# A convolution and a routed FFN on one core: weights ahead of the first rows, small scale operations on GpSimd, routing of the first chunks sooner

## The chip, the core and the metric

The kernel runs on one core of one Trainium2 chip. The core has TensorE (PE, matrix products), VectorE (DVE), ScalarE (ACT) and GpSimd (POOL), each with a queue that it works off in order, and SyncE (SP), which issues most DMA transfers. PSUM is where TensorE leaves its products, SBUF the memory that all engines work in. The metric is the device time of one execution in microseconds (us); less is better.

## The reference

A softmax over 7 weights per head forms a causal convolution of x; its output goes through a layer of 8 experts of which each row uses one.

```python
# attention-like convolution: B, S, D = 8, 3584, 192; 8 heads; K = 7
w = np.exp(weight_gen - weight_gen.max(-1, keepdims=True)); w /= w.sum(-1, keepdims=True) + 1e-9
out = np.einsum('bshk,bskhg->bshg', w, x_unf)      # 7 shifted rows of x per row
x = out.reshape(28672, 192)
# experts: w1 (8, 192, 1024), w2 (8, 1024, 192)
logits = x @ w_gate
expert_idx = np.argmax(logits, axis=1)
gate_w = softmax(logits)[row, expert_idx]
for e in range(8):
    h = np.maximum(x[expert_idx == e] @ w1[e], 0)
    out[expert_idx == e] = gate_w * (h @ w2[e])
```

## The kernel before

**Chunks.** The rows are taken in 16 chunks of up to 14 tiles of 128 rows. conv(c) forms a chunk on VectorE by multiplications (L358) and additions (L363) of two SBUF operands; soft_a and soft_b (L302 to L341) do its softmax, size_a (L312, ScalarE) and size_b (L322, GpSimd) find a power of two by which the chunk is scaled. The rows are then split into two fp16 halves: the upper by ScalarE (tops, L372), the lower by VectorE (halves, L384). TensorE transposes them (turn, L398; ScalarE copies them out, L399) and multiplies them by the router's weights (products, L407).

**Routing.** route1(s) (VectorE, L419 to L437) picks each row's expert and leaves counts per expert in cnt; its first operation, fac (L419), is the factor that undoes the scaling. counts(s) issues ScalarE's Exp (L445) and TensorE's two sums of counts (L446, L447). route2(s) (VectorE, L468 to L482) computes pos, the place of each row in a list sorted by expert, and its 14 scatters (L457, GpSimd, DMA_INDIRECT scr<-rows,pos) write the rows to a buffer in DRAM. VectorE then builds small tables of blocks (L494 to L534).

**Preparation of the experts' weights.** Each expert's weights are scaled by powers of two from their size and split into fp16 parts: sq (L184, ScalarE, squares), total (L232, TensorE, sums over partitions), scales (L234: scale_of, L171 to L180, four small operations on VectorE: eb, ei, ws, wi), high (L244 si, L246 wt, ScalarE), low (TensorE L256, L257, ScalarE L258) and store (SyncE, L266 to L273, to wsc in DRAM). prep_units() lists these units in order, and prepare(t, ta) issues those that are due by time t.

**FFN.** The sorted rows are worked through in blocks of 256 rows, 7 blocks per stage; stage s can begin when the scatters of some chunk have landed. load() has SyncE issue the first weights (L563, L564), the transposed rows x (L571, which waits for the stage's scatters), mt (L579) and the second weights (L590). Per block TensorE does the first products (L611 to L615), ScalarE takes hh (L618), VectorE the remainder hl (L628; in early stages ScalarE, L626), TensorE the second products (L644), ScalarE scales them to y (L651), and GpSimd writes y to the output by two indirect DMAs (L652, DMA_INDIRECT out_dram<-y,mt).

**Order.** VectorE, ScalarE, TensorE and SyncE work in the order in which two coroutines issue instructions: produce() (chunks, routing, preparation) and consume() (FFN). Each holds an estimated time; t and ta are those of VectorE and ScalarE, avail[s] is the time from which a stage's blocks may be issued, and whichever coroutine is behind goes next. The tables FIRST, SECOND, THIRD, EARLY and STEADY say behind which of a chunk's 13 convolution operations (-1 to 13) each part of the work on the chunk before is issued; SECOND holds for the work on chunk 1, THIRD for chunk 2. GpSimd's order is made by the scheduler from what was issued, with priorities. In load(), the first block of all took x ahead of its first weights, the others behind them.

Of the kernel before, what the change touches and what calls it, by code (L numbers as in the profile page):

```python
# [7 lines left out]
F32 = mybir.dt.float32  # L8
# [4 lines left out]
ALU = mybir.AluOpType  # L13
AX = mybir.AxisListType

P = 128
# [23 lines left out]
THIRD = dict(tops=-1, halves=0, turn=1, per=2, products=3, route1=5, counts=6, route2=7, soft_a=8, soft_b=10, size=11)  # L40
SECOND = dict(tops=-1, halves=-1, turn=-1, per=6, products=-1, route1=-1, counts=-1, route2=0, soft_a=6, soft_b=10, size=8)
# [38 lines left out]
def conv_moe_kernel(ctx: ExitStack, tc: tile.TileContext, x, wgen, wg_in, w1, w2, out):  # L80
# [90 lines left out]
    def scale_of(ss, s_out, i_out, by=GP):  # L171


        n = ss.shape[1]
        eb = small.tile([P, 4], F32, name="eb", bufs=4)
        ei = small.tile([P, 4], I32, name="ei", bufs=4)
        by.tensor_scalar(out=eb[:, 0:n], in0=ss.bitcast(I32), scalar1=11.0 * 2 ** 23, scalar2=-(2.0 ** -24), op0=ALU.max, op1=ALU.mult)
        by.tensor_scalar(out=ei[:, 0:n], in0=eb[:, 0:n], scalar1=190 - 2.0 ** -8, scalar2=None, op0=ALU.add)
        by.tensor_scalar(out=s_out.bitcast(I32), in0=ei[:, 0:n], scalar1=2.0 ** 23, scalar2=None, op0=ALU.mult)
        by.tensor_scalar(out=i_out.bitcast(I32), in0=s_out.bitcast(I32), scalar1=-1.0, scalar2=254.0 * 2 ** 23, op0=ALU.mult, op1=ALU.add)  # L180
# [39 lines left out]
    def prep_units():  # L220
# [13 lines left out]
        def scales(e):  # L234
            with tc.high_priority(offset=PRIO3):
                scale_of(sqs.pop(e)[0][:, 0:2], ws[:, 2 * e:2 * e + 2], wi[:, 2 * e:2 * e + 2], V)
# [85 lines left out]
    def size_b(c):  # L322
        ll = tin[c]["ll"]
        sx = small.tile([P, 4], F32, name="sx", bufs=4)
        tin[c]["new"] = ll[:, 0:1]
        if WID[c] > 7:
            GP.tensor_tensor(out=ll[:, 3:4], in0=ll[:, 0:1], in1=ll[:, 1:2], op=ALU.add)
            tin[c]["new"] = ll[:, 3:4]
        GP.tensor_tensor(out=sx[:, 0:1], in0=tin[c]["new"], in1=tin[c - 1]["new"] if c else ll[:, 2:3], op=ALU.add)
        scale_of(sx[:, 0:1], sx[:, 1:2], sx[:, 2:3])  # L330
        tin[c]["sx"] = sx
# [81 lines left out]
    def route1(s):  # L413
# [3 lines left out]
        with tc.high_priority(offset=PRIO2):  # L417
            fac = small.tile([P, 1], F32, name="fac")
            V.tensor_scalar(out=fac, in0=d["sx"][:, 2:3], scalar1=wi[:, 2 * E:2 * E + 1], scalar2=None, op0=ALU.mult)  # L419
# [21 lines left out]
    def counts(s):  # L441
        d = seg[s]
        d["pc"] = pc = d["pl"][:, 496:512]
        with tc.high_priority(offset=PRIO2):
            A.activation(out=d["lg"], in_=d["lg"], func=AF.Exp, scale=d["fac"])  # L445
            PE.matmul(pc[:, 0:E], lhsT=tri, rhs=d["cnt"], start=True, stop=True)  # L446
            PE.matmul(pc[:, E:16], lhsT=ones, rhs=d["cnt"], start=True, stop=True)  # L447

# [103 lines left out]
    def load(s, tb, g, bs):  # L552
# [8 lines left out]

        def firsts():
            SP.dma_start(out=wt[:, F:4 * F], in_=wsc[bass.ds(ev, 1), :, F:4 * F].rearrange("o p c -> p (o c)"))  # L563
            SP.dma_start(out=wt[0:64, 0:F], in_=wsc[bass.ds(ev, 1), 0:64, 0:F].rearrange("o p c -> p (o c)"))  # L564

        ahead_of_rows = bool(loaded)
        if ahead_of_rows:
            firsts()
# [7 lines left out]
        if not ahead_of_rows:  # L576
            firsts()
# [117 lines left out]
    def produce():  # L695
# [23 lines left out]
        for c in range(nchunk + 1):  # L719
# [4 lines left out]
            for o in range(-1, OPS + 1):  # L724
# [63 lines left out]
                if o == -1 and c == 2:  # L788
                    ta = prepare(ta + 1.0, ta)
# [4 lines left out]
                if o == at_o["counts"] and c:  # L794
                    counts(c - 1)
# [7 lines left out]
                ta = prepare(t - 2.5 if c == 1 and o > 10 else t, ta)  # L803
# [110 lines left out]
```

## Time and profile before

| | |
|---|---|
| time, median of 3 runs | 1248.54 us (1246.06 to 1250.6) |
| the profiled execution | 1246.52 us, of which the span 1244.7 us |
| PE busy | 1124.1 us, 90% of the span |
| DVE busy | 1061.7 us, 85% |
| POOL busy | 809.0 us, 65% |
| ACT busy | 705.7 us, 57% |
| DMA | 323.03 MB, 260 GB/s on average |

The busy shares are means over very different stretches: preparation and the first chunks up to about 158 us, then convolution and FFN side by side, and from about 967 us on mostly FFN. Starts are counted from the beginning of the span. A row of a timeline gives start, duration, engine, line of the kernel, operation, what it writes and reads, and in brackets how long the engine was idle ahead of it and whose work ended that.

### The profile page before, as it was taken

The page shows a single profiled execution, that of the slowest core. Times are in us where ns is not written, and L with a number is a line of the kernel's source. Part 1 is how long each engine was busy: PE and PEld are TensorE (multiplying, and loading weights), DVE is VectorE, ACT ScalarE, POOL GpSimd, SP SyncE. Part 2 cuts the span into 40 slices and gives each one's busy share as a digit, 9 for nine tenths or more (in the row PEclk, how much of TensorE's full clock was granted, in tenths as well). Part 3 has the DMA queues.
Part 4 walks back from the last instruction along what each step waited for, and adds up shares of the span by engine and source line. Part 5 has one row for each costly group of instructions (what it writes and reads, how often), then busy time and mean ns, then how long its engine had stood idle before and what let it go on. Part 6 is the DMA issues. An engine that isn't in the chain of part 4 may idle for free. (4 is left out here: it accounts for less than half of the span.)

```text
span 1244.7 us, 31113 instructions
## 1 busy us (share of the span) xinstructions
PE 1124.1 (90%) x11784; PEld 1010.3 (81%) x11784; DVE 1061.7 (85%) x1421; ACT 705.7 (57%) x1299; POOL 809.0 (65%) x611
## 2 busy tenths in 40 slices
PE   1665499899998999999999999999998999999997
PEld 0233178788887898889999999998998899999996
DVE  8999999999999999999999999999999865333332
ACT  5968765767776766645555455555545354334332
POOL 3227615858889898888888888886858573522222
PEclk9867899899999999999999999999999999999999
DMA  9749697796978999999999999999995999999992
GB/s 326 208 151 317 225 313 213 223 262 222 308 204 262 243 280 255 301 241 287 285 298 293 272 316 260 320 281 262 268 275 173 286 245 280 307 296 249 256 243 73
DMA packets 211945, 323.03 MB, mean 260 GB/s; under 512 B 138894, under 2 KB 158463, under 8 KB 209744
## 3 DMA queue, kind: packets, MB, share of 16 engines
q1 hardware_dynamic: 190000, 276.01, 80.4%
q0 software_dynamic: 21792, 44.99, 11.6%
q8 instruction: 94, 1.54, 0.5%
q14 instruction: 59, 0.48, 0.1%
HBM read 237.87 MB, written 61.03 MB: 240 GB/s over the span
## 5 line engine op out<-in xcount | busy, mean ns | idle before, releaser
L652 POOL DMA_INDIRECT out_dram<-y,mt x230 | 349.7, 1521 | 275.9 <-ACT y L651 215.9
L618 ACT ACTIVATE hh<-p 128x512 f16<-128x512 f32 x460 | 275.7, 600 | 381.3 <-PE p L615 360.0
L457 POOL DMA_INDIRECT scr<-rows,pos x224 | 373.5, 1667 | 100.7 <-issue 60.0
L644 PE MATMUL po<-wt,hh 128*128 128x192 f16 x3680 | 363.8, 247 | 0.0
L628 DVE SCALAR_TENSOR_TENSOR hl<-p,hh 128x512 f16<-128x512 f32 x334 | 225.0, 680 | 138.7 <-ACT hh L618 138.6
L644 PEld LDWEIGHTS <-hh 128*128 128x128 f16 x3680 | 313.4, 98 | 3.3
L358 DVE TENSOR_TENSOR tmp<-xin,wgt 128x1344 f32<-128x1344 f32 (+1 forms) x168 | 290.7, 1746 | 1.0
L363 DVE TENSOR_TENSOR acc<-acc,tmp 128x1344 f32<-128x1344 f32 (+1 forms) x168 | 290.6, 1747 | 1.0
L611 PE MATMUL p<-xb,wt 128*128 128x256 f16 x920 | 252.0, 274 | 31.8 <-DMA wt<-wsc 18.7
L614 PE MATMUL p<-xb,wt 128*128 128x256 f16 x920 | 252.4, 274 | 0.0
L613 PE MATMUL p<-xb,wt 128*128 128x256 f16 x920 | 252.3, 274 | 0.0
L612 PE MATMUL p<-xb,wt 128*128 128x256 f16 x920 | 252.3, 274 | 0.0
L615 PE MATMUL p<-xb,wt 128*128 128x256 f16 x920 | 252.2, 274 | 0.0
L644 PE MATMUL po<-wt,hl 128*128 128x192 f16 x1840 | 227.7, 247 | 8.2 <-DVE hl L628 8.2
L644 PEld LDWEIGHTS <-hl 128*128 128x128 f16 x1840 | 163.9, 98 | 18.5 <-DVE hl L628 10.7
L611 PEld LDWEIGHTS <-wt 128*128 128x128 f16 x920 | 90.3, 98 | 42.4 <-issue 35.6
L626 ACT ACTIVATE hl<-p 128x512 f16<-128x512 f32 x126 | 76.1, 604 | 50.5 <-PE p L625 49.2
L612 PEld LDWEIGHTS <-wt 128*128 128x128 f16 x920 | 90.3, 98 | 16.9 <-issue 1.4
L399 ACT ACTIVATE xt<-p 128x1024 f16<-128x1024 f16 x96 | 86.9, 928 | 23.3 <-PE p L398 21.9
L614 PEld LDWEIGHTS <-wt 128*128 128x128 f16 x920 | 90.5, 98 | 11.1
L615 PEld LDWEIGHTS <-wt 128*128 128x128 f16 x920 | 90.6, 98 | 11.0
L613 PEld LDWEIGHTS <-wt 128*128 128x128 f16 x920 | 90.5, 98 | 11.0
(123 smaller groups left out, 1057.3 us busy)
## 6 DMA issues: line engine op xcount, KB each, us to landing
wt<-wsc SPq DMA_DIRECT2D x115, 768.5 KB
wt<-wsc SPq DMA_DIRECT2D x115, 768.0 KB
xin<-in_x_dram SPq DMA_DIRECT2D x15, 1344.0 KB
wt<-wsc SPq DMA_DIRECT2D x115, 128.0 KB
wgt<-in_weight_gen_dram SPq DMA_DIRECT2D x16, 392.0 KB
wsc<-wt SPq DMA_DIRECT2D x8, 768.5 KB
wa<-in_moe_w_dram SPq DMA_DIRECT2D x8, 768.0 KB
wa<-in_moe_w_dram SPq DMA_DIRECT2D x8, 512.0 KB
```

Source lines behind the costliest of these rows:

```text
L358: V.tensor_tensor(out=t[:, a:b, :].rearrange("p t (h g) -> p (t h) g", g=G), in0=xv, in1=wv, op=ALU.mult)
L363: V.tensor_tensor(out=acc[:, a:b, :], in0=acc[:, a:b, :], in1=t[:, a:b, :], op=ALU.add)
L457: i = raw(GP.indirect_dma_start(scri, bass.IndirectOffsetOnAxis(ap=pos[:, t:t + 1], axis=0), rows_t[s % 3].bitcast(I32)[:, t, 0:RW // 2], ...
L611: PE.matmul(o, lhsT=wt[:, F + fs:F + fs + P], rhs=xv[:, 0, :], start=i == 0, stop=False)
L612: PE.matmul(o, lhsT=wt[:, F + fs:F + fs + P], rhs=xv[:, 1, :], start=False, stop=False)
L613: PE.matmul(o, lhsT=wt[:, 3 * F + fs:3 * F + fs + P], rhs=xv[:, 0, :], start=False, stop=False)
L614: PE.matmul(o, lhsT=wt[:, 2 * F + fs:2 * F + fs + P], rhs=xv[:, 2, :], start=False, stop=False)
L615: PE.matmul(o, lhsT=wt[:, fs:fs + P], rhs=xv[:, 2, :], start=False, stop=i == self.each - 1)
L618: A.activation(out=hh, in_=p1, func=AF.Relu, scale=1.0 - 2.0 ** -11 if self.via[k] else 1.0)
L628: V.scalar_tensor_tensor(out=hl, in0=p1, scalar=0.0, in1=hh, op0=ALU.max, op1=ALU.subtract)
L644: PE.matmul(o, lhsT=h[:, js], rhs=w2, start=(f == 0 and j % 2 == 0 and not part and w == 0), stop=part == 1 and f == NF - 1 and (j % 2 == ...
L652: i = raw(GP.indirect_dma_start(out, bass.IndirectOffsetOnAxis(ap=self.mt[:, j, 1:2], axis=0), y, None, bounds_check=N - 1, oob_is_err=False))
```

## The change

1. The tables: for chunk 2 (THIRD) route1, counts and route2 come one step sooner; for chunk 1 (SECOND) route2 comes at -1, as counts does.
2. scale_of takes another engine, then, for all but its first operation. For experts 0 to 3 the last three (ei, ws, wi) go to GpSimd; the first reads PSUM and stays on VectorE.
3. size_b computes fac for chunks from 1 on, on GpSimd; route1 computes it on VectorE for chunk 0 alone.
4. counts takes a function, between, which for chunk 1 issues the units of preparation that were issued ahead of it before: now behind ScalarE's Exp and, on TensorE, ahead of the sums of counts. While chunk 0 is routed, prepare is called twice with t + 4, so units are issued earlier there; at the end of conv(1) it is called with t - 1.5 instead of t - 2.5.
5. load() issues the first weights ahead of x in every block, the first one included.

```diff
--- before.py
+++ after.py
@@ -37,8 +37,8 @@
 STEADY = dict(tops=0, halves=2, turn=3, per=1, products=8, route1=10, counts=12, route2=13, soft_a=4, soft_b=7, size=10)
 FIRST = dict(tops=-1, halves=0, turn=0, per=6, products=1, route1=3, counts=3, route2=4, soft_a=6, soft_b=10, size=8)
 EARLY = dict(tops=-1, halves=1, turn=2, per=2, products=4, route1=6, counts=8, route2=9, soft_a=7, soft_b=10, size=11)
-THIRD = dict(tops=-1, halves=0, turn=1, per=2, products=3, route1=5, counts=6, route2=7, soft_a=8, soft_b=10, size=11)
-SECOND = dict(tops=-1, halves=-1, turn=-1, per=6, products=-1, route1=-1, counts=-1, route2=0, soft_a=6, soft_b=10, size=8)
+THIRD = dict(tops=-1, halves=0, turn=1, per=2, products=3, route1=4, counts=5, route2=6, soft_a=8, soft_b=10, size=11)
+SECOND = dict(tops=-1, halves=-1, turn=-1, per=6, products=-1, route1=-1, counts=-1, route2=-1, soft_a=6, soft_b=10, size=8)
 END = 2.1
 QUICK = (2, 3, 4)
 WB = 4
@@ -168,13 +168,14 @@
         rows_t.append(r)
 
 
-    def scale_of(ss, s_out, i_out, by=GP):
+    def scale_of(ss, s_out, i_out, by=GP, then=None):
 
 
         n = ss.shape[1]
         eb = small.tile([P, 4], F32, name="eb", bufs=4)
         ei = small.tile([P, 4], I32, name="ei", bufs=4)
         by.tensor_scalar(out=eb[:, 0:n], in0=ss.bitcast(I32), scalar1=11.0 * 2 ** 23, scalar2=-(2.0 ** -24), op0=ALU.max, op1=ALU.mult)
+        by = then or by
         by.tensor_scalar(out=ei[:, 0:n], in0=eb[:, 0:n], scalar1=190 - 2.0 ** -8, scalar2=None, op0=ALU.add)
         by.tensor_scalar(out=s_out.bitcast(I32), in0=ei[:, 0:n], scalar1=2.0 ** 23, scalar2=None, op0=ALU.mult)
         by.tensor_scalar(out=i_out.bitcast(I32), in0=s_out.bitcast(I32), scalar1=-1.0, scalar2=254.0 * 2 ** 23, op0=ALU.mult, op1=ALU.add)
@@ -233,7 +234,7 @@
 
         def scales(e):
             with tc.high_priority(offset=PRIO3):
-                scale_of(sqs.pop(e)[0][:, 0:2], ws[:, 2 * e:2 * e + 2], wi[:, 2 * e:2 * e + 2], V)
+                scale_of(sqs.pop(e)[0][:, 0:2], ws[:, 2 * e:2 * e + 2], wi[:, 2 * e:2 * e + 2], V, GP if e < 4 else None)
 
         wts, stored = {}, {}
 
@@ -328,6 +329,8 @@
             tin[c]["new"] = ll[:, 3:4]
         GP.tensor_tensor(out=sx[:, 0:1], in0=tin[c]["new"], in1=tin[c - 1]["new"] if c else ll[:, 2:3], op=ALU.add)
         scale_of(sx[:, 0:1], sx[:, 1:2], sx[:, 2:3])
+        if c:
+            GP.tensor_scalar(out=sx[:, 3:4], in0=sx[:, 2:3], scalar1=wi[:, 2 * E:2 * E + 1], scalar2=None, op0=ALU.mult)
         tin[c]["sx"] = sx
 
     def soft_b(c):
@@ -415,8 +418,9 @@
         n = WID[s]
         pl = d["pl"]
         with tc.high_priority(offset=PRIO2):
-            fac = small.tile([P, 1], F32, name="fac")
-            V.tensor_scalar(out=fac, in0=d["sx"][:, 2:3], scalar1=wi[:, 2 * E:2 * E + 1], scalar2=None, op0=ALU.mult)
+            fac = d["sx"][:, 3:4]
+            if s == 0:
+                V.tensor_scalar(out=fac, in0=d["sx"][:, 2:3], scalar1=wi[:, 2 * E:2 * E + 1], scalar2=None, op0=ALU.mult)
             lg = work.tile([P, T, E], F32, name="lg")[:, 0:n, :]
             V.tensor_reduce(out=lg, in_=pl[:, 0:16 * n].rearrange("p (t z e) -> p t e z", z=2, e=E), axis=AX.X, op=ALU.add)
             lm = small.tile([P, n], F32, name="lm")
@@ -438,13 +442,15 @@
         d.update(lg=lg, oh=oh, inc=inc, cnt=cnt, fac=fac)
         yield 1.1
 
-    def counts(s):
+    def counts(s, between):
         d = seg[s]
         d["pc"] = pc = d["pl"][:, 496:512]
         with tc.high_priority(offset=PRIO2):
             A.activation(out=d["lg"], in_=d["lg"], func=AF.Exp, scale=d["fac"])
+            ta = between() if s == 1 else None
             PE.matmul(pc[:, 0:E], lhsT=tri, rhs=d["cnt"], start=True, stop=True)
             PE.matmul(pc[:, E:16], lhsT=ones, rhs=d["cnt"], start=True, stop=True)
+        return ta
 
     def no_dep(i, *groups):
         for g in groups:
@@ -558,14 +564,8 @@
         wt = wts[len(loaded2) % len(wts)]
         loaded2.append(None)
         seconds()
-
-        def firsts():
-            SP.dma_start(out=wt[:, F:4 * F], in_=wsc[bass.ds(ev, 1), :, F:4 * F].rearrange("o p c -> p (o c)"))
-            SP.dma_start(out=wt[0:64, 0:F], in_=wsc[bass.ds(ev, 1), 0:64, 0:F].rearrange("o p c -> p (o c)"))
-
-        ahead_of_rows = bool(loaded)
-        if ahead_of_rows:
-            firsts()
+        SP.dma_start(out=wt[:, F:4 * F], in_=wsc[bass.ds(ev, 1), :, F:4 * F].rearrange("o p c -> p (o c)"))
+        SP.dma_start(out=wt[0:64, 0:F], in_=wsc[bass.ds(ev, 1), 0:64, 0:F].rearrange("o p c -> p (o c)"))
         xb = ffn.tile([P, 3 * 512], F16, name="xb", bufs=3)
         xv = xb[:, 0:3 * bs].rearrange("p (a b) -> p a b", a=3)
         i = raw(SP.dma_start_transpose(out=xv, in_=scr[bass.ds(rv, bs), 0:384]))
@@ -573,8 +573,6 @@
         no_dep(i, *later)
         written(i, s)
         tc.add_to_no_dep_group("loads", i)
-        if not ahead_of_rows:
-            firsts()
         mt = ffn.tile([P, 2, 2], I32, name="mt", bufs=16)
         i = raw(SP.dma_start(out=mt[:, 0:nj, :], in_=scri[bass.ds(rv, bs), 192:194].rearrange("(j p) c -> p j c", p=P)))
         no_dep(i, *later)
@@ -785,14 +783,14 @@
                         for d in soft_b(c + 1):
                             t += d
                             yield t
-                if o == -1 and c == 2:
-                    ta = prepare(ta + 1.0, ta)
+                if c == 1 and o in (1, 2):
+                    ta = prepare(t + 4, ta)
                 if o == at_o["route1"] and c:
                     for d in route1(c - 1):
                         t += d
                         yield t
                 if o == at_o["counts"] and c:
-                    counts(c - 1)
+                    ta = counts(c - 1, lambda: prepare(ta + 1.0, ta)) or ta
                 if o == at_o["route2"] and c:
                     for d in route2(c - 1):
                         t += d
@@ -800,7 +798,7 @@
                     avail[c - 1] = t + state["own"] + 1.7 * WID[c - 1] + AV
                 if o < 0 and c != 2:
                     continue
-                ta = prepare(t - 2.5 if c == 1 and o > 10 else t, ta)
+                ta = prepare(t - 1.5 if c == 1 and o > 10 else t, ta)
                 yield t
         state["done"] = True
         yield 1e9
```

GpSimd's queue around the scatters of chunk 13, before. L177 to L180 are size_b's operations for chunk 15, L652 an output of half a block, and L457 the 14 scatters:

```order
L652 DMA out_dram<-y,mt 28672x192 x8
L327 TENSOR_TENSOR ll<-ll 128x1
L329 TENSOR_TENSOR sx<-ll 128x1
L177 TENSOR_SCALAR eb<-sx 128x1
L178 TENSOR_SCALAR ei<-eb 128x1
L179 TENSOR_SCALAR sx<-ei 128x1
L180 TENSOR_SCALAR sx<-sx 128x1
L652 DMA out_dram<-y,mt 28672x192 x2
L457 DMA scr<-rows_138,pos 231680x200 x14
L652 DMA out_dram<-y,mt 28672x192 x14
```

The same place in the changed kernel:

```order
L650 DMA out_dram<-y,mt 28672x192 x8
L328 TENSOR_TENSOR ll<-ll 128x1
L330 TENSOR_TENSOR sx<-ll 128x1
L177 TENSOR_SCALAR eb<-sx 128x1
L179 TENSOR_SCALAR ei<-eb 128x1
L180 TENSOR_SCALAR sx<-ei 128x1
L181 TENSOR_SCALAR sx<-sx 128x1
L650 DMA out_dram<-y,mt 28672x192
L333 TENSOR_SCALAR sx<-sx,wi 128x1
L650 DMA out_dram<-y,mt 28672x192 x3
L463 DMA scr<-rows_138,pos 231680x200 x14
L650 DMA out_dram<-y,mt 28672x192 x12
```

Ahead of the scatters stand 160 outputs in all where 158 stood; for chunk 12 they are 144 and 142, for chunks 8 and 9 also two more, and for the other chunks as many as before.

GpSimd's queue at the start of conv(0), before: gate's scale (gmr) and chunk 0's (sx), then size_b of chunk 1:

```order
L177 TENSOR_SCALAR eb<-gmr 128x1
L180 TENSOR_SCALAR sx<-sx 128x1
L178 TENSOR_SCALAR ei<-eb 128x1
L179 TENSOR_SCALAR ws<-ei 128x1
L180 TENSOR_SCALAR wi<-ws 128x1
L327 TENSOR_TENSOR ll<-ll 128x1
```

In the changed kernel, where 128x2 marks an expert's scales (here expert 0; those of experts 1 and 2 follow in the same form ahead of size_b of chunk 1):

```order
L177 TENSOR_SCALAR eb<-gmr 128x1
L181 TENSOR_SCALAR sx<-sx 128x1
L179 TENSOR_SCALAR ei<-eb 128x1
L180 TENSOR_SCALAR ws<-ei 128x1
L181 TENSOR_SCALAR wi<-ws 128x1
L179 TENSOR_SCALAR ei<-eb 128x2
L180 TENSOR_SCALAR ws<-ei 128x2
L181 TENSOR_SCALAR wi<-ws 128x2
```

The three operations of expert 0, which VectorE did, now stand in GpSimd's queue behind the gate's, and ScalarE's si for expert 0 waits for them.

ScalarE's queue where chunk 0 is routed, before (lg is the Exp of counts(0); si, wt and the three wt from PSUM are units of preparation):

```order
L399 ACTIVATE xt<-p_514 128x256
L184 ACTIVATE junk,wsq<-wa 128x1536
L445 ACTIVATE lg<-lg,fac 128x112
L244 ACTIVATE si<-idf,ws 128x128
L246 ACTIVATE wt<-wa,ws 128x1536
L258 ACTIVATE wt<-p_592 128x512
```

And in the changed kernel:

```order
L402 ACTIVATE xt<-p_515 128x256
L185 ACTIVATE junk,wsq<-wa 128x1536
L245 ACTIVATE si<-idf,ws 128x128
L247 ACTIVATE wt<-wa,ws 128x1536
L259 ACTIVATE wt<-p_571 128x512
L259 ACTIVATE wt<-p_575 128x512
L259 ACTIVATE wt<-p_579 128x512
L449 ACTIVATE lg<-lg,sx 128x112
```

si, wt and three parts from PSUM have moved ahead of the Exp.

## Rows read from the trace of the kernel before

**Rows 1.** Busy time by stretch: PE, PEld, DVE, ACT, POOL, clock, DMA, GB/s.

```profile
160.00:931.00 771.00, 746.24 (x8203) 687.74 (x8202) 756.27 (x973) 460.88 (x866) 602.71 (x395) 0.99 0.96 269
...
967.00:1225.00 258.00, 257.94 (x2801) 243.69 (x2800) 119.46 (x222) 106.62 (x223) 96.43 (x93) 0.99 1.01 266
```

**Rows 2.** Timeline of PE: first matmuls of stages 1, 2, 4, 12, 13.

```profile
158.26 0.37 PE L611 MATMUL p<-xb,wt 128*128 128x256 f16 x1 [18.73 <-DMA wt<-wsc]
...
230.68 0.37 PE L611 MATMUL p<-xb,wt 128*128 128x256 f16 x1 [3.53 <-DMA xb<-scr]
...
381.46 0.27 PE L611 MATMUL p<-xb,wt 128*128 128x256 f16 x1 [1.54 <-DMA xb<-scr]
...
897.95 0.27 PE L611 MATMUL p<-xb,wt 128*128 128x256 f16 x1
...
966.49 0.37 PE L611 MATMUL p<-xb,wt 128*128 128x256 f16 x1 [6.13 <-DMA xb<-scr]
```

**Rows 3.** Timeline of SP's queue: x loads of stages 12 and 13.

```profile
891.40 1.37 SPq L571 DMA_TRANSPOSE xb<-scr  x1
...
963.27 1.26 SPq L571 DMA_TRANSPOSE xb<-scr  x1
```

**Rows 4.** Timeline of POOL: first and last of 14 scatters of chunk 13.

```profile
931.93 0.97 POOL L457 DMA_INDIRECT scr<-rows,pos  x1 [2.16 <-DVE pos L482]
...
958.56 3.23 POOL L457 DMA_INDIRECT scr<-rows,pos  x1 [0.30 <-issue]
```

**Rows 5.** Timeline of DVE: positions of chunks 10, 12 and 13.

```profile
711.95 0.34 DVE L482 TENSOR_REDUCE pos<-inc 128x14 int32<-128x112 f32 x1
...
858.38 0.35 DVE L482 TENSOR_REDUCE pos<-inc 128x14 int32<-128x112 f32 x1
...
931.31 0.34 DVE L482 TENSOR_REDUCE pos<-inc 128x14 int32<-128x112 f32 x1
```

**Rows 6.** Timeline of ACT: y of the blocks behind these positions.

```profile
719.09 0.74 ACT L651 ACTIVATE y<-po,g 128x192 f32<-128x192 f32 x2
...
862.77 0.73 ACT L651 ACTIVATE y<-po,g 128x192 f32<-128x192 f32 x2
...
934.24 0.73 ACT L651 ACTIVATE y<-po,g 128x192 f32<-128x192 f32 x2
```

**Rows 7.** Timeline of POOL: first and last of 14 scatters of chunk 10.

```profile
725.93 1.75 POOL L457 DMA_INDIRECT scr<-rows,pos  x1 [0.30 <-issue]
...
754.66 1.76 POOL L457 DMA_INDIRECT scr<-rows,pos  x1 [0.30 <-issue]
```

**Rows 8.** Timeline of POOL: first and last of 14 scatters of chunk 12.

```profile
859.00 0.98 POOL L457 DMA_INDIRECT scr<-rows,pos  x1 [1.38 <-DVE qi L495]
...
884.95 1.76 POOL L457 DMA_INDIRECT scr<-rows,pos  x1 [0.30 <-DMA xb<-scr]
```

**Rows 9.** Timeline of DVE and POOL in conv(0): gate's scales beside convolution.

```profile
28.43 1.55 DVE L363 TENSOR_TENSOR acc<-acc,tmp 128x1344 f32<-128x1344 f32 x1
28.57 1.49 POOL L178 TENSOR_SCALAR ei<-eb 128x1 int32<-128x1 f32 x1
...
30.02 1.56 DVE L358 TENSOR_TENSOR tmp<-xin,wgt 128x1344 f32<-128x1344 f32 x1
...
30.15 1.50 POOL L179 TENSOR_SCALAR ws<-ei 128x1 int32<-128x1 int32 x1
```

**Rows 10.** Timeline of ACT: expert 0's first si, and Exp of chunk 0.

```profile
28.64 0.39 ACT L244 ACTIVATE si<-idf,ws 128x128 f32<-128x128 f32 x1
...
75.32 0.39 ACT L445 ACTIVATE lg<-lg,fac 128x112 f32<-128x112 f32 x1 [5.20 <-DVE vr L426]
```

**Rows 11.** Timeline of DVE: scales of expert 4, fac, halves of chunk 2.

```profile
83.36 0.16 DVE L177 TENSOR_SCALAR eb<-po 128x2 f32<-128x2 int32 x1 [1.82 <-PE po L232]
...
118.47 0.22 DVE L419 TENSOR_SCALAR fac<-sx,wi 128x1 f32<-128x1 f32 x1
...
174.97 2.08 DVE L384 SCALAR_TENSOR_TENSOR rows<-acc,sx,rows 128x1792 f16<-128x1792 f32 x1 [1.06 <-ACT rows L372]
```

**Rows 12.** Busy time by stretch, as rows 1, behind stage 2's first matmul.

```profile
230.00:235.00 5.00, 4.32 (x24) 3.52 (x25) 5.00 (x4) 2.82 (x4) 4.53 (x6) 0.50 0.89 281
```

## The prediction

> **What bounds the kernel now.** I read the busy time by stretch first. From 160 to 931 us TensorE is busy 746 of 771 us and VectorE 756, so both nearly set the pace; from 967 to 1225 TensorE is busy 257.94 of 258 [rows 1]. After 967 nothing waits, so the end is a constant behind TensorE's restart there. The next view is TensorE's timeline at the starts of stages: at 966.49 it had stood for 6.13 us on the x of stage 13, at 230.68 for 3.53 (stage 2), at 381.46 for 1.54 (stage 4), and at 897.95 (stage 12) not at all [rows 2]. SyncE's queue says when those x loads went out: 963.27 for stage 13, so 3.2 us from load to first matmul, but 891.40 for stage 12, which leaves 6.55 us, 3.3 more than it needs [rows 3]. A stage's x load waits for the last of the 14 scatters of its chunk. GpSimd's timeline shows these for chunk 13: first at 931.93, right behind the positions of 931.31, last at 958.56 for 3.23 us [rows 4, 5]. So the end of the kernel is: positions of chunk 13, its scatters, x load, restart, constant. What delays the scatters of chunk 13 delays the end in full; those of chunk 12 have 3.3 us of room.
>
> The profiled execution took 1246.52 us (span 1244.7), 2.0 below the median of 1248.54. I make the sum against the former and add 2.0.
>
> **The part that I weigh most: what stands ahead of the scatters on GpSimd.** The planner puts FFN work half a block sooner relative to the convolution. On GpSimd the scatters of chunks 12 and 13 now stand behind four output DMAs where they stood behind two; the later two belong to one more block. An output needs that block's y. ScalarE makes those y at 862.77 and 934.24, ending 0.73 us later, at 863.5 and 934.97 [rows 6], while the positions are there at 858.7 and 931.65 [rows 5]. GpSimd's queue runs in order, so the scatters wait for y, then for two outputs.
> The kernel before already shows this case once: at chunk 10 four outputs stand ahead. Positions come at 711.95, the block's y at 719.09, the first scatter at 725.93 and the last at 754.66 [rows 5 to 7]: 14 us from positions to first scatter, where chunks 12 and 13 have 0.6 [rows 4, 5, 8]. It costs nothing at chunk 10, whose FFN work is needed only later.
> Two things add up. The start moves to y plus two outputs of 1.28 us (0.97 and a gap of 0.30, as the scatter at 931.93 [rows 4]). And the stretch in which VectorE builds its small tables, where scatters go at 1.28, goes to the outputs, so all 14 go at the rate of chunk 10: (754.66 - 725.93) / 13 = 2.21 us [rows 7], 30.9 for 14. Chunk 13 itself, with four quick ones, gives 26.6 / 13 = 2.05 as the lower bound; its other nine steps, (26.6 - 5.1) / 9 = 2.39, the upper.
>
> **The early parts, as a shift P of TensorE at stage 4.** Whatever happens before stage 4 reaches stage 12 only as a common shift, since stages 3 and 4 start on their x.
> *Scales by GpSimd.* Twelve operations of 0.16 us (as at 83.36 [rows 11]) leave VectorE: -1.9. But at 28.57 and 30.15 GpSimd's one-column operations take 1.49 and 1.50 us; the first ends with the VectorE TENSOR_TENSOR that started at 28.43 [rows 9]. Expert 0's three now stand behind the gate's on GpSimd: five held operations and its own first, each at a step of 1.59 (30.02 - 28.43), make 9.5; from 28.1 on (28.57 less the 0.5 by which VectorE's operation now starts sooner) that is 37.6. Its second falls under a one-input operation. ScalarE's first si, at 28.64 [rows 10], waits for that second: 9 us later. Bounds: 0 if nothing is held, 11.1 if seven are. I take 9, because the rows shown are the same operations in the same place. ScalarE has 5.20 us without work at 75.32 [rows 10], which the change fills (high and low parts of two experts go there); VectorE's waits of 1.82 at 83.36 and 1.06 at 174.97 vanish when it is itself late [rows 11]. P = 9.0 - 5.2 - 1.8 - 1.1 = +0.9. VectorE's 1.9 goes into waits for the late ScalarE. If nothing is held, P = -1.9 - 1.8 - 1.1 = -4.8. Upper bound, if only ScalarE's gap takes part of it up: 9.0 - 5.2 = +3.8.
> The Trainium skill, "SBUF — State Buffer", section "SBUF: two separate sides", says that VectorE with two SBUF inputs and a GpSimd operation that reads SBUF exclude each other for a whole instruction, whichever starts first. The trace agrees on GpSimd's side. By that rule the twelve operations could also hold VectorE when they start first, 12 x 0.2 = 2.4 us more; no row here shows such a hold, and the sum goes without it.
> *fac on GpSimd.* Fifteen operations of 0.22 us at most go from VectorE [rows 11]: 3.3 us by the end, 0.7 by stage 4. GpSimd gets one small operation per chunk, in time it idles. It doesn't help where y, not positions, is awaited.
> *Chunk 1's positions right behind counts, chunk 2's routing a pair sooner.* The first takes one convolution operation out of the way (1.55, as at 28.43 [rows 9]), the second two, about 3.1. They move x of stages 1 and 2; stage 2 then loses some of its 3.53 [rows 2]. Stages 3 and 4 start on later x loads, so nothing of it stays in P. Counts for TensorE directly behind the products: between -2 and +1 on stage 1, likewise gone.
> *Weights ahead of the first x.* TensorE starts at 158.26 on weights [rows 2]; with x issue to matmul 3.2 it gains at most 5 us, and the stand at stage 2 takes it back. The same swap for the conditional block at the very end costs nothing, since its loads go out during the block before. On SyncE the load of chunk 3 moves behind five stores; two chunks of convolution cover it. Without the cover VectorE would wait for those few issues, some us, inside the bounds of P.
>
> **The sum, P = +0.9.** Stage 12: y 863.5 + 0.9 = 864.4, two outputs 867.0, scatters 897.9, x load 1.5 later as at stage 13 (961.79 to 963.27 [rows 3, 4]; 886.71 to 891.40, 4.7, at stage 12 is the upper bound [rows 3, 8]; I take 1.5 since TensorE again stands) 899.4, first matmul 902.6 instead of 897.95: +4.7. TensorE would have been there at 898.85, so it stands 3.8 us. After the similar stand before 230.68 the granted clock of the next 5 us was 0.50 [rows 12], the lower of two levels: half of 5, +2.5. Shift +7.2. Stage 13: y 934.97 + 7.2 = 942.2, outputs 944.8, scatters 975.7, x load 977.2, first matmul 980.4 instead of 966.49: **+13.9**. Its low clock after the stand is in the time before already. Behind it TensorE is full [rows 1], so the end moves by as much: 1246.5 + 13.9 = 1260.4, and 2.0 for the median: **1262**.
> Bounds: P = -4.8 and a step of 2.05 give stage 12 894.7 (stand 1.6, no clock taken off), stage 13 967.7: +1.2, a median of 1250. P = +3.8, 2.39 and 4.7 give +25, 1274.
>
> **Rivals.** *A. Both stages are held*, as above: 1262, from 1258 to 1270. For it: chunk 10's rows. Against: TensorE's stand at stage 12 could be shorter if P is small.
> *B. Stage 12 absorbs its part; only 13 is held.* It needs the scatters of chunk 12 done by about 894, which a step of 2.05 gives from 865 on. Then stage 13 alone: 934.97 + 0.9 + 2.6 + 30.9 + 1.5 + 3.2 = 974.1, +7.6: 1256.
> *C. The FFN really runs nearly half a block sooner*, because GpSimd isn't held early and x of stages 2 to 4 come sooner: the low bound, 1250. For it: stands of 3.53 and 1.54 that could give way [rows 2]. Against: the held rows [rows 9].
> *D. Faster: FFN gains all that the planner gives it.* If the first matmuls come 5 us sooner, the stands at stages 2 and 4 don't take it back and the held operations don't occur, P is near -8: y of stage 13 is there at 927, about when VectorE, 4.8 sooner, has the positions, and the two outputs fit into the 2.16 us in which GpSimd idles there [rows 4]. Then the end follows VectorE: -4.8, 1244. It decides from P = -8 on, 3 us beyond the bound above; against it stand the x loads of stages 3 and 4, and I leave it a chance because P is a sum of differences of a few us each.
> That the change doesn't do what it says is in A: the twelve operations leave VectorE and come back as waits.
>
> **How the numbers follow.** A 0.62, B 0.14, C 0.12, D 0.12. 0.3% (3.7 us) is about what a measurement of this kernel can tell from no change; A and B lie above, C within, D below: slower 0.76, same 0.12, faster 0.12. The likeliest is A, 1262. The range 1249 to 1270 leaves out D, a little of C and the top of A's bound, together some 0.2.
>
> **What would show it.** Right: in the changed kernel's GpSimd timeline the outputs ahead of the scatters of chunks 12 and 13 wait for ScalarE's y, and the first scatter comes 4 us or more behind the positions; TensorE stands before stage 12, where it didn't, and about 14 us or more before stage 13; GpSimd's early operations take 1.4 to 1.6 us and ScalarE's first si comes near 37. Wrong: scatters of chunk 13 within 1 us of their positions (then D or C), an early si near 29 (then P is negative), or a TensorE that waits after 980.

## The result: slower, by half of what was forecast

The changed kernel takes 1254.5 us (median of 5 runs, 1254.04 to 1255.52) where the kernel before takes 1247.92 in the runs beside it: 6.6 us more, a ratio of 1.0052 (95% interval 1.004 to 1.0065). The profiled execution took 1254.41 us, its span is 1252.5, 7.8 longer than before's 1244.7. The traced execution of the kernel before (1246.52) lies 1.4 below its median, so the traces differ by a little more than the medians. Twelve of the runs told below (e1 to e4, e9 to e16) fell on three disturbed chips, on which the kernel before itself took 1313 to 1383 us; of these only what their traces show up to 130 us is used.

The starts of blocks on TensorE show where the 7.8 us come from; a stand is a time in which TensorE waits. Timeline of PE, changed kernel, first matmuls of stages 4, 12, 13, of the second block of stage 13 and of the last block but one of stage 14 (block 96, counted from 0); they answer to [rows 2]:

```profile
382.64 0.37 PE L609 MATMUL p<-xb,wt 128*128 128x256 f16 x1 [3.39 <-DMA xb<-scr]
...
897.18 0.27 PE L609 MATMUL p<-xb,wt 128*128 128x256 f16 x1 [2.81 <-DMA xb<-scr]
...
971.03 0.37 PE L609 MATMUL p<-xb,wt 128*128 128x256 f16 x1 [12.41 <-DMA xb<-scr]
...
983.21 0.27 PE L609 MATMUL p<-xb,wt 128*128 128x256 f16 x1 [0.60 <-ACT xt L402]
...
1081.83 0.27 PE L609 MATMUL p<-xb,wt 128*128 128x256 f16 x1 [2.86 <-DMA xb<-scr]
```

Stage 4 starts 1.18 us later than before, stage 12 0.77 sooner, stage 13 4.54 later after a stand twice as long as before's 6.13. The second block of stage 13 is 5.03 later, and that holds up to block 95. At block 96 TensorE stands again, where before it didn't, and from there on everything is 7.8 later. So the loss has two places: the x load of stage 13, and something new at block 96. SyncE's queue names both (timeline of SP, changed kernel: x of stage 13, the eight zero fills for the last chunk, x of block 96):

```profile
967.91 1.27 SPq L571 DMA_TRANSPOSE xb<-scr  x1
...
1064.42 8.76 SPq L532 DMA_DIRECT2D scr<-zrow  x8
...
1075.99 1.34 SPq L571 DMA_TRANSPOSE xb<-scr  x1
```

x of stage 13 goes out 4.64 us later than in [rows 3]. The fills, which write the empty rows behind each expert's list, now stand ahead of x of block 96; in the kernel before they stood behind it (timeline of SP, kernel before: x of block 96, fills, x of block 97):

```profile
1060.37 1.34 SPq L571 DMA_TRANSPOSE xb<-scr  x1
...
1063.18 8.58 SPq L526 DMA_DIRECT2D scr<-zrow  x8
...
1075.16 1.44 SPq L571 DMA_TRANSPOSE xb<-scr  x1
```

On GpSimd the outputs of blocks 71 and 79 stand ahead of the scatters, as the order said. Timeline of POOL, changed kernel, in two stretches: the output that waits for y and the first scatter of chunk 12; an output of block 79, first and last scatter of chunk 13. They answer to [rows 4, 8]:

```profile
860.16 0.98 POOL L650 DMA_INDIRECT out_dram<-y,mt  x1 [4.48 <-ACT y L649]
861.45 0.98 POOL L650 DMA_INDIRECT out_dram<-y,mt  x1 [0.31 <-issue]
862.73 0.97 POOL L463 DMA_INDIRECT scr<-rows,pos  x1 [0.30 <-DVE hl L626]
...
933.20 0.98 POOL L650 DMA_INDIRECT out_dram<-y,mt  x1 [0.46 <-ACT y L649]
934.48 0.99 POOL L650 DMA_INDIRECT out_dram<-y,mt  x1 [0.30 <-issue]
935.78 0.98 POOL L463 DMA_INDIRECT scr<-rows,pos  x1 [0.30 <-DVE hl L626]
...
965.17 1.16 POOL L463 DMA_INDIRECT scr<-rows,pos  x1 [0.30 <-issue]
```

Positions and y, timelines of DVE and ACT of the changed kernel, answer to [rows 5, 6]:

```profile
859.47 0.73 ACT L649 ACTIVATE y<-po,g 128x192 f32<-128x192 f32 x2
...
859.96 0.34 DVE L488 TENSOR_REDUCE pos<-inc 128x14 int32<-128x112 f32 x1
...
932.51 0.72 ACT L649 ACTIVATE y<-po,g 128x192 f32<-128x192 f32 x2
...
932.72 0.34 DVE L488 TENSOR_REDUCE pos<-inc 128x14 int32<-128x112 f32 x1
```

The positions are 1.58 and 1.41 us later than before, but the y are 3.30 and 1.73 sooner. They come together, so the scatters wait for little more than the two outputs: they start 3.73 (chunk 12) and 3.85 us (chunk 13) later than before.

The early part went as the row on GpSimd's holds said [rows 9, 10]. Timeline of POOL (gate's scale, then ei and ws of expert 0) and of ACT, changed kernel:

```profile
27.96 1.47 POOL L177 TENSOR_SCALAR eb<-gmr 128x1 f32<-128x1 int32 x1
29.50 1.48 POOL L181 TENSOR_SCALAR sx<-sx 128x1 int32<-128x1 int32 x1
...
35.66 1.56 POOL L179 TENSOR_SCALAR ei<-eb 128x2 int32<-128x2 f32 x1
37.30 0.23 POOL L180 TENSOR_SCALAR ws<-ei 128x2 int32<-128x2 int32 x1
...
37.57 0.40 ACT L245 ACTIVATE si<-idf,ws 128x128 f32<-128x128 f32 x1 [8.87 <-POOL ws L180]
```

Six operations of one or two columns take 1.36 to 1.56 us each, and ScalarE begins with expert 0 at 37.57 instead of 28.64. Two new waits carry that to VectorE (timeline of DVE, changed kernel: scales of expert 2, halves of chunk 0):

```profile
47.12 0.16 DVE L177 TENSOR_SCALAR eb<-po 128x2 f32<-128x2 int32 x1 [3.90 <-PE po L233]
...
66.38 3.15 DVE L387 SCALAR_TENSOR_TENSOR rows<-acc,sx,rows 128x1792 f16<-128x1792 f32 x2 [2.93 <-ACT rows L375]
```

### The profile page after: what moved, and what is told of

Its sections match the earlier page's. It is cut to its first block, busy times and chain, and to the rows that moved or that the text cites. A ratio compares the mean times of both kernels' runs of the same rounds, so it can differ in the third digit from the quotient of the medians.

```text
span 1252.5 us, 31131 instructions
## 1 busy us (share of the span) xinstructions
PE 1125.3 (90%) x11784; PEld 1011.0 (81%) x11784; DVE 1058.3 (84%) x1394; ACT 705.2 (56%) x1299; POOL 818.9 (65%) x638
## 5 line engine op out<-in xcount | busy, mean ns | idle before, releaser
L650 POOL DMA_INDIRECT out_dram<-y,mt x230 | 332.9, 1447 | 278.8 <-ACT y L649 219.3
L463 POOL DMA_INDIRECT scr<-rows,pos x224 | 368.9, 1647 | 84.5 <-issue 58.4
```

The lines of the kernel that those rows point to most:

```text
L463: i = raw(GP.indirect_dma_start(scri, bass.IndirectOffsetOnAxis(ap=pos[:, t:t + 1], axis=0), rows_t[s % 3].bitcast(I32)[:, t, 0:RW // 2], ...
L650: i = raw(GP.indirect_dma_start(out, bass.IndirectOffsetOnAxis(ap=self.mt[:, j, 1:2], axis=0), y, None, bounds_check=N - 1, oob_is_err=False))
```

## The experiments

My theory after the result had two terms, both from the table THIRD, which moves FFN work half a block sooner: outputs stand ahead of scatters, and zero fills ahead of block 96. Undoing THIRD was to give back nearly the whole loss. The rival was expert 0's scales, which wait in GpSimd's queue (VectorE's 3.90 and 2.93); my theory put their price at a microsecond or less. Other rivals were that the outputs only stand in the same place as the loss, or that each place gives way to the next. Each of the three terms has an edit of its own.

Each kernel is compared with the kernel before on the same chip; that took 1248.12 us beside e5 to e8 and 1247.58 beside e17 and e18.

| run | what it is | us | ratio to before (95% interval) |
|---|---|---|---|
| the change | | 1254.50 | 1.0052 (1.004 to 1.0065) |
| e5 | outputs behind the scatters | 1253.97 | 1.0043 (1.0027 to 1.0059) |
| e6 | that, and zero fills one load later | 1250.74 | 1.0016 (1.0005 to 1.0026) |
| e7 | THIRD undone | 1250.08 | 1.0015 (1.0004 to 1.0026) |
| e18 | expert 0's scales on VectorE | 1247.94 | 1.0009 (0.9998 to 1.002) |
| e8 | THIRD undone, all scales on VectorE | 1245.15 | 0.9982 (0.9971 to 0.9992) |
| e17 | THIRD undone, expert 0's scales on VectorE | 1243.17 | 0.9964 (0.9953 to 0.9976) |

### Outputs behind the scatters (e1, e5)

The outputs of two blocks are held and issued behind the last scatter of the chunk; PE, DVE, ACT and SP keep their order.

```diff
+        if s in BEHIND.values():
+            flush(scats[s][-1])
...
+    held, done, BEHIND = [], [0], {71: 12, 79: 13}
+    def flush(behind=None):
+        while held:
+            mt, j, y = held.pop(0)
+            with tc.issue_after(behind) if behind else ExitStack():
+                i = raw(GP.indirect_dma_start(out, ...))
...
-                i = raw(GP.indirect_dma_start(out, ...))
...
+                held.append((self.mt, j, y))
+            b = BEHIND.get(done[0])
+            if b is None or len(scats.get(b, ())) == T:
+                flush(scats[b][-1] if b else None)
+            done[0] += 1
```

Expected of e1:

> The changed kernel with one edit: the outputs of blocks 71 and 79 are queued on GpSimd behind the scatters of chunks 12 and 13, as in the kernel before (142 and 158 outputs ahead instead of 144 and 160); nothing else moves on any engine. Theory (the outputs hold the scatters): the scatters of chunk 13 start within 0.6 us of their positions, about 933 instead of 935.78, four of them at 1.28 us, and end near 963.3 instead of 966.33; the x load of stage 13 goes out near 965 instead of 967.91, the stand of 2.81 us at stage 12 goes, and the time is 3 us shorter, about 1251.5. Rival (the scatters are late because positions and VectorE are late, and the outputs are only in the same place): at most the 0.3 us of one gap, 1254.2; the rate of the scatters gives back what the earlier start wins.

Expected of e5, the same kernel on an undisturbed chip:

> The kernel of e1 again, on a chip that isn't disturbed: the outputs of blocks 71 and 79 behind the scatters of chunks 12 and 13, nothing else moved. Theory (the outputs hold the scatters): the scatters of chunk 13 start within 0.6 us of their positions, x of stage 13 goes out near 965 instead of 967.91, the stand at stage 12 goes, and the time is 3 us shorter than the changed kernel's, about 1251.5 where the kernel before takes 1248. Rival (the outputs only stand in the same place, VectorE is what is late): 1254.2.

The mechanism is as expected, the time isn't: 1253.97, a ratio lower by 0.0009, about 1 us, inside both intervals. Timeline of the run over all engines (positions and first scatter of chunk 13, stage 13, fills, x and first matmul of block 96):

```profile
932.86 0.34 DVE L488 TENSOR_REDUCE pos<-inc 128x14 int32<-128x112 f32 x1
933.49 0.97 POOL L463 DMA_INDIRECT scr<-rows,pos  x1 [1.76 <-DVE pos L488]
...
967.96 0.37 PE L623 MATMUL p<-xb,wt 128*128 128x256 f16 x1 [10.95 <-DMA xb<-scr]
...
1062.31 9.69 SPq L534 DMA_DIRECT2D scr<-zrow  x8
...
1074.76 1.27 SPq L573 DMA_TRANSPOSE xb<-scr  x1
...
1079.92 0.37 PE L623 MATMUL p<-xb,wt 128*128 128x256 f16 x1 [3.07 <-DMA xb<-scr]
```

Stage 13 starts at 967.96, 3.07 us sooner than in the changed kernel, the scatters start 0.63 us behind their positions, and the stand at stage 12 falls from 2.81 to 0.87. But 1.0 of it is gone by the next block, and block 96 stands for 3.07 us again, since the fills ahead of its x took 9.69 us. Behind this stand the granted clock was low; in the changed kernel, behind a stand of 2.86, it wasn't (busy time by stretch with the clock, then DMA share and GB/s, at the end: the changed kernel, then e5):

```profile
1081.00:1086.00 5.00, 4.17 (x46) 4.01 (x47) 0.69 (x1) 0.60 (x1) 1.42 (x2) 1.00 1.03 392
```

```profile
1079.00:1084.00 5.00, 4.08 (x23) 3.40 (x24) 0.69 (x1) 0.60 (x1) 1.32 (x2) 0.50 1.05 404
```

So the place at stage 13 is real and worth 3 us there. In this execution the gain is lost again behind it, mostly by the clock: 1.0 us in the first block of stage 13 (granted 0.50 from 968 to 973, where the changed kernel had 0.68 from 971 to 976), 0.2 at the fills, and 2.8 in block 96, which takes 11.15 us instead of 8.32. That the other executions lost theirs in the same way isn't shown.

### Zero fills one load later (e2, e3, e6)

```diff
-                for e in range(E):
-                    v = SP.value_load(ni[0:1, e:e + 1], ...)
-                    i = raw(SP.dma_start(out=scri[bass.ds(v, 256), :]...))
...
+                fills.append(ni)
...
         loaded.append(i)
         halfway.append((wt, ev))
+        fill()
```

fill() issues the eight value loads and fills that stand with a minus.

Expected of e2, this edit alone:

> The changed kernel with one edit: the eight zero fills of the last chunk on SyncE's queue (8.8 us of issues at 1064.42) stand behind the loads of block 96 instead of ahead of them, as in the kernel before. Theory (they cost the 2.86 us that TensorE stands at block 96): x of block 96 goes out about 1064.5 instead of 1075.99, no stand there, and the time is 2.9 us shorter, about 1251.6. Rival (the fills hold whichever load is behind them, so the stand moves to block 97): 1254 to 1254.5, with a stand of 2 to 3 us at block 97.

Expected of e6, both edits:

> As e5, and the zero fills of the last chunk one load later on SyncE. If the zero fills are a term of their own: 2.9 us below e5, about 1248.6. If TensorE's stand moves to the next load: as e5.

e6 takes 1250.74, 3.2 below e5, and x of block 96 no longer waits. The stand moves on to block 97, as the rival said. Timeline of e6 over all engines (fills, x and first matmul of block 97):

```profile
1065.85 10.54 SPq L549 DMA_DIRECT2D scr<-zrow  x8
...
1079.89 1.37 SPq L580 DMA_TRANSPOSE xb<-scr  x1
...
1087.96 0.37 PE L631 MATMUL p<-xb,wt 128*128 128x256 f16 x1 [3.34 <-DMA xb<-scr]
```

The first x behind the fills is late in either place. In these two traces the stand is no shorter one load further back (3.34 us against 3.07), and e6's span is 1.5 us shorter by the clock: the block behind the stand took 9.91 us instead of 11.15, the first block of stage 13 12.38 instead of 13.13. The traced execution of e6 took 1253.77, 3.0 above its median, so its trace doesn't explain the 3.2 us. The edit alone (e2, repeated as e9 and e13) and both (e3) gave no time that can be used, so the value of the fills without the other edit isn't measured.

### THIRD undone (e7), and scales on VectorE besides (e8)

```diff
-THIRD = dict(..., route1=4, counts=5, route2=6, ...)
+THIRD = dict(..., route1=5, counts=6, route2=7, ...)
```

Expected of e7:

> The changed kernel with the table of chunk 2 (THIRD) as before, all other parts of the change kept. The order then has 142 and 158 outputs ahead of the scatters of chunks 12 and 13 and the zero fills behind the loads of block 96. Theory (the loss of 6 to 8 us is what that one table moves late in the program, in GpSimd's and SyncE's queues): 1247.5 to 1250, and the positions of chunk 13 come later than before by less than 1.4 us. Rival (the loss comes from expert 0's scales and the late ScalarE): 1252 to 1254.5, since these are kept.

e8 also has

```diff
-                scale_of(sqs.pop(e)[0][:, 0:2], ..., V, GP if e < 4 else None)
+                scale_of(sqs.pop(e)[0][:, 0:2], ..., V)
```

> As e7, and all scale operations on VectorE as before; weights ahead of the first x, fac on GpSimd, the preparation in ScalarE's gap and chunk 1's positions behind its counts are kept. Theory: ScalarE's first si near 28.6; VectorE has 1.5 to 4 us less than before by chunk 13, which decides stage 13's x load, so 1244 to 1247. Rival (GpSimd's scales are worth their place, the gap takes the 9 us up): as e7 or 1 us above.

e7 gives 1250.08, at the upper edge of the theory: 142 and 158 outputs stand ahead again, the scatters of chunk 13 start 0.61 us behind their positions, and 4.4 us come back (0.0037 in ratio). Its positions of chunk 13 are 1.0 us later than before. Timelines of e7 (first scatter of chunk 13; first matmul of block 97):

```profile
932.93 0.97 POOL L463 DMA_INDIRECT scr<-rows,pos  x1 [2.23 <-DVE pos L488]
...
1086.71 0.27 PE L609 MATMUL p<-xb,wt 128*128 128x256 f16 x1 [1.97 <-DMA xb<-scr]
```

The fills stand behind x of block 96 again, and TensorE still waits behind them, at block 97: 1.97 us here, 2.11 in e8 and 1.78 in e17, where the kernel before has no such wait. So undoing THIRD takes off about 1 us of the stand at the fills, and its trace gains most at stage 13, which starts 3.42 us sooner than in the changed kernel. In the kernel before block 97 began 8.55 us behind block 96, where a block without a wait takes 8.32, so its x came with no time to spare; which part of the change takes that last room isn't known. e6, which keeps THIRD and moves only outputs and fills, takes nearly the same as e7 (1250.74), so no further price of THIRD shows.

e8 takes off 4.9 more and is faster than the kernel before. So neither cause is the whole.

### Which of the scales (e4, e10 to e12, e14 to e18)

```diff
-                scale_of(sqs.pop(e)[0][:, 0:2], ..., V, GP if e < 4 else None)
+                scale_of(sqs.pop(e)[0][:, 0:2], ..., V, GP if 0 < e < 4 else None)
```

On the disturbed chips, first: e4 is the changed kernel with this edit, e10 (and e14) has all scales on VectorE, e11 (and e15) this edit with THIRD undone.

> The changed kernel with one edit: all four scale operations of expert 0 on VectorE, as before; experts 1 to 3 keep three of theirs on GpSimd. ScalarE's first si comes at about 28.6 instead of 37.57. Theory A (the 9 us of ScalarE are taken up in its own gaps and move VectorE by 1 to 3 us; at stage 13 the scatters wait for y and its outputs): positions of chunk 13 earlier by 1 to 3 us, the scatters by less than 1, time 1253.5 to 1254.5. Rival B (that late start is the cause of the loss): positions and scatters both 3 us or more earlier, time 1251 or below.

> The changed kernel with all scale operations on VectorE as before, everything else kept (THIRD too). e8 less e7 was -4.9 us without THIRD. Theory (GpSimd's scales cost VectorE 4 to 5 us by chunk 13, by ScalarE's late start, but with the outputs ahead of the scatters y decides): positions of chunk 13 near 928, the scatters follow y and two outputs, near 933; time 1250 to 1252.5, less than the 4.9 of e8. Rival (the scales are the whole loss, the order late in the program costs nothing): 1249 to 1250.

> As e7 (THIRD undone), with the scales of expert 0 alone on VectorE; experts 1 to 3 keep three operations each on GpSimd. If the cost of GpSimd's scales is expert 0's place behind the gate's operations: as e8 or a little below, 1244.5 to 1246, ScalarE's first si near 28.6. If each expert's scales cost by their holds: between e8 and e7, 1246.5 to 1249, with waits of ScalarE's si for GpSimd at experts 1 and 2.

Up to 130 us these traces agree with those of the undisturbed chips, and the positions of chunk 1 fall in three groups: with expert 0's scales on GpSimd 125.0 to 126.3 us (nine runs, the changed kernel's 125.04 the first of them), with all scales on VectorE 120.7 to 121.7 (five, e8 at 120.74), with expert 0 alone on VectorE 118.9 to 119.8 (five). So expert 0's place costs 6 to 7 us there, and the nine operations of experts 1 to 3 are 1.4 to 1.9 us well spent on GpSimd. The times of e10 (ratio 1.004, 0.9961 to 1.0119) and e14 (0.9923, 0.9837 to 1.001), one kernel, tell nothing; nor do the others there, which lie from 0.9749 (e15) to 0.9987 (e9): one kernel came out at 0.9963 as e1 and at 1.0043 as e5.

e12 (and e16) keeps THIRD, with all scales on VectorE, the outputs behind the scatters and the fills one load later:

> The changed kernel with THIRD kept, scales on VectorE, outputs of blocks 71 and 79 behind the scatters and zero fills one load later. If THIRD only does harm by these two queues, it is worth what e8 is: 1245 to 1246; if half a block's sooner FFN gives something, 1242 to 1244.5; if it does harm elsewhere, 1247 or above.

0.9934 (0.9869 to 0.9999) and 0.9872 (0.9801 to 0.9944) there, so whether THIRD is worth something once its two places are undone and the scales are on VectorE stays open.

On an undisturbed chip:

> THIRD undone and the scales of expert 0 alone on VectorE. In the disturbed runs positions of chunk 1 came at 119.4 to 119.8 us with this placing, 120.7 to 121.2 with all scales on VectorE and 125.0 to 125.9 with GpSimd's. If these leads last to chunk 13, 1.2 us below e8: 1243.5 to 1244.5. If they are lost in between: 1245 to 1246.

> The changed kernel with one edit, the scales of expert 0 on VectorE; THIRD kept. If y and the outputs hold the scatters of chunk 13 whatever VectorE does, at most half of the 5 to 6 us that VectorE gains is seen: 1251 to 1252.5. If the stage follows VectorE: 1248.5 to 1250.

e18, another engine for three operations, gives back the loss: 1247.94, and a ratio of 1.0009 that can't be told from 1. The difference of the ratios, 0.0043, is 5.4 us, as the second expectation had it (the stage follows VectorE). It does so with both places of THIRD kept: the first scatter of chunk 13 (928.44) stands behind two outputs, 1.75 us behind its positions, and block 96 waits for 3.07 us. e17 gives 1243.17, 4.4 us below the kernel before (0.9964, 0.9953 to 0.9976); it is the fastest of the kernels in the table. Timeline of e18 over all engines (positions of chunks 1 and 13, stage 13, block 96):

```profile
118.89 0.34 DVE L488 TENSOR_REDUCE pos<-inc 128x14 int32<-128x112 f32 x1
...
926.69 0.34 DVE L488 TENSOR_REDUCE pos<-inc 128x14 int32<-128x112 f32 x1
...
963.50 0.37 PE L609 MATMUL p<-xb,wt 128*128 128x256 f16 x1 [12.66 <-DMA xb<-scr]
...
1074.57 0.27 PE L609 MATMUL p<-xb,wt 128*128 128x256 f16 x1 [3.07 <-DMA xb<-scr]
```

The same of e17 (first si; positions and first scatter of chunk 13; stage 13):

```profile
28.82 0.39 ACT L245 ACTIVATE si<-idf,ws 128x128 f32<-128x128 f32 x1
...
925.44 0.34 DVE L488 TENSOR_REDUCE pos<-inc 128x14 int32<-128x112 f32 x1
926.05 0.97 POOL L463 DMA_INDIRECT scr<-rows,pos  x1 [2.23 <-DVE pos L488]
...
960.62 0.37 PE L609 MATMUL p<-xb,wt 128*128 128x256 f16 x1 [6.22 <-DMA xb<-scr]
```

In e18 the positions of chunk 1 are 6.15 us sooner than in the changed kernel (125.04), those of chunk 13 6.03, stage 13 7.53, and the traced span ends 7.3 sooner: what chunk 1 loses is still there at the end. From e18 to e17, THIRD undone, the positions of chunk 13 gain 1.25 (two hl operations fewer ahead of them), the start of stage 13 2.88, and the end 3.4.

The four kernels with and without the two causes fit together: the ratio falls by 0.0043 (expert 0) and 0.0037 (THIRD) singly and by 0.0088 with both. The spans of their traces (1252.5, 1245.2, 1249.1, 1241.8) say the same: 7.3 and 3.4 us singly, 10.7 with both. The two causes add. Without them the rest of the change is a gain of 0.0036.

## Why the prediction was right in kind and wrong in size

**The sign and the places.** Slower was right, and the chain that the prediction followed is the one that decides: positions, two outputs, scatters, x load, stage 13, with a new stand at stage 12. Rival D's conditions did not occur, and the early si came at 37.57 where 37.6 was worked out. Of the prediction's own signs, the outputs that wait for y (4.48 us at chunk 12, 0.46 at chunk 13), the stand at stage 12 and the early operations came as said; the scatters started 2.77 and 3.06 us behind the start of their positions, not 4 or more, the stand at stage 13 was 12.41, not 14, and one sign of being wrong occurred: TensorE waited after 980.

**The nearest rival.** The number is nearest to rival B (1256): the scatters of chunk 12 were done by 891.63, within its 894, and stage 12 passed on nothing. B's stage 13 came out at 974.1 where 971.03 was measured, 3.1 too late, since it too took y 0.9 us later than before instead of 1.73 sooner; that its total is only 1.5 off is luck, since it has no stand at block 96.

**P.** +0.9 at stage 4 was the sum, +1.18 was measured. The net was right; that it is made of a large loss and gains nearly as large shows only in e18: with expert 0 on VectorE stage 4 starts at 376.19, 6.5 us sooner. The sum treated ScalarE's gap and VectorE's waits as taking the 9 us up. They are taken up, but they were also what the other parts of the change would have won; with expert 0 on VectorE these are worth 5.3 us at stage 4 (376.19 against 381.46).

**The step that failed.** "Whatever happens before stage 4 reaches stage 12 only as a common shift": y of blocks 71 and 79 were put at their times of before plus P. They came 3.30 and 1.73 us sooner than before instead of 0.9 later and, through the loss at stage 12, 7.2 later. The half block by which the plan moves FFN ahead was counted in GpSimd's queue, where it puts outputs ahead of scatters, and not on TensorE, where the blocks themselves then run sooner against the work on chunks. Timelines of PE, first matmul of block 71, in the kernel before, the changed kernel and e7:

```profile
845.71 0.27 PE L611 MATMUL p<-xb,wt 128*128 128x256 f16 x1
```

```profile
841.43 0.27 PE L609 MATMUL p<-xb,wt 128*128 128x256 f16 x1
```

```profile
846.80 0.27 PE L609 MATMUL p<-xb,wt 128*128 128x256 f16 x1
```

TensorE started block 71 4.28 us sooner than before, though stage 4 had begun 1.18 later, and with THIRD undone (e7) 1.09 later: the lead is THIRD's. So the comparison with chunk 10 [rows 5 to 7], whose scatters waited 14 us, was too dear: y and positions came 0.5 and 0.2 us apart. The sum was +13.9 at stage 13 and measures +4.54. Of the 9.4 us between them 8.0 lie at stage 12: it was to pass on a shift of 7.2, and it began 0.8 sooner than before.

**Its parts.** The two outputs cost what they were put at: 933.20 to 935.78 is 2.6 us. The step of the scatters of chunk 13 was (965.17 - 935.78) / 13 = 2.26, against 2.21. The stand at stage 12 was 2.81, not 3.8, and the clock there stayed up (granted 1.00 from 897 to 902), so the 2.5 us for it fell away. The 4.54 is made of 1.41 by which the positions are later, 2.44 by which the first scatter stands further behind them (3.06 against 0.62), and 0.69 by which the 14 scatters take longer (30.55 against 29.86). Another 0.5 is lost in the block behind, where TensorE waits 0.60 for ScalarE's xt.

**What was missed.** "After 967 nothing waits, so the end is a constant behind TensorE's restart": true of the kernel before, not of the changed one. The zero fills move by one load on SyncE, by the same half block, and TensorE stands for 2.86 us at block 96. The prediction followed GpSimd's queue to stage 13 and SyncE's only early in the program. This stand is the last 2.8 us of the 7.8. Only about 1 us of it goes with THIRD, since e7, e8 and e17 still wait 1.8 to 2.1 us behind the fills; where the rest comes from stays open.

**Parts at nothing.** Weights ahead of the first x: the first matmul came at 153.85, 4.4 sooner, and stage 2 stood for 6.28 us instead of 3.53; the gain is taken back there, as the prediction said. The routing of chunk 2 a pair sooner brought its positions 1.9 us forward, but its 14 scatters took 24.67 us instead of 21.68, and stage 2 began 0.95 later. fac, the preparation in ScalarE's gap and the order of the first load weren't tried singly.

**GpSimd and VectorE.** Six GpSimd operations in a row took 1.36 to 1.56 us beside VectorE's two-input operations, as the sum had them, and with the nine operations of experts 1 to 3 on GpSimd VectorE was 1.4 to 1.9 us sooner at chunk 1, not later. Its step from one two-input operation to the next is 1.59 us beside GpSimd's operations (from 29.38 to 30.97) and 1.59 without them (from 53.56 to 55.15). The Trainium skill, "SBUF — State Buffer", section "SBUF: two separate sides", has either engine held by the other, whichever starts first: the trace agrees for GpSimd, and the up to 2.4 us that VectorE might have lost by that rule don't show.

## What to carry to other kernels

The price of a small operation that is moved to another queue is its place there: three operations of a fifth of a microsecond cost 6 to 7 us at chunk 1 since they stood behind five that are held by the neighbour, and the engine they feed had nothing else to do; the same operations for the next experts were a gain. When a plan moves work by half a block, all engines' queues have to be read for what changed places, up to the end of the program, and the moved work's own times change with them: neither the price in one queue nor the times of before may be kept. A gain ahead of a place that also waits for something else must be followed to the next such place before it is counted.

## What the runs showed that was not expected

A loss at 37 us, before any FFN work, was still there in full 1200 us later (6.15 us at chunk 1, 7.3 at the end of the traced executions), through stands of TensorE that could have taken it up: the stands follow VectorE's chunks, and VectorE is busy for 756 of 771 us [rows 1]. And two stands of one length, 3.07 us ahead of block 96 in e5 and in e18, were followed by a granted clock of 0.50, the lower of the two levels, in e5, which made block 96 take 11.15 us instead of 8.32, and by 1.00 in e18 (busy time by stretch, as above, e18):

```profile
1074.00:1079.00 5.00, 4.43 (x48) 4.24 (x49) 0.69 (x1) 0.60 (x1) 0.98 (x1) 1.00 1.07 385
```

So the length of the stand alone doesn't decide the clock behind it.
